# Five score blocks of an attention kernel exponentiated on GpSimd as powers of two

## The chip, the cores and the metric

The kernel runs on one core of a Trainium2 chip. The metric is device time in microseconds (us) from launch to end. The engines named here are TensorE (PE: matrix products; PEld is its weight load), ScalarE (ACT: exponentials), VectorE (DVE: elementwise work), GpSimd (POOL: its own small instructions and some DMA issues) and SyncE (SP: most DMA issues). Each engine runs its own list of instructions strictly in order; semaphores tie the lists together. SBUF is the on-chip working memory of 128 partitions, PSUM the memory that TensorE writes, with eight banks of 128x512 fp32.

## What is computed

Two independent blocks over a sequence of 2048 rows and 512 channels, joined along the last axis.

```python
# A: attention with 32 heads of 16 channels
qkv = x @ wqkv
scores = einsum("bhqd,bhkd->bhqk", q, k) * (Dh ** -0.5)
p = softmax(scores)
a = einsum("bhqk,bhkd->bhqd", p, v) ... @ wo
# B: a 4-tap shift, a gate, a causal convolution as long as the sequence, a gate
kv = (k shifted and weighted by shift_k) * v
y = causal_conv(kv, ssm_k) + kv * ssm_D      # the reference does it by FFT
b = q * y
return concatenate([a, b], axis=-1)
```

The softmax is computed without subtracting a maximum: a row of exponentials is multiplied with the values and with a column of ones, and the sum that the ones give divides the result.

## The kernel before, in words

**Score blocks.** The 2048 x 2048 scores of 32 heads are cut into 2048 blocks of 128 keys by 512 queries (`NBLK`). A block is one matmul of 32 rows (`emit_qk`, L730) into one PSUM bank. Four heads that lie in the four 32-row strips of TensorE, at one block of queries, form a *head group*: 64 blocks, numbered one after another; there are 32 groups (`blk_group`). Scores leave TensorE already multiplied by log2(e) and by 2^16 (`QSCALE`, `OCT`), so a block needs 2 to the power score/2^16.

**Chunks.** Blocks are taken in chunks of two or three. Chunk T uses three PSUM banks, 0 to 2 or 3 to 5 by turns, so chunk T+2 needs the banks of chunk T back. One activation on ScalarE (L737) turns a whole chunk into bf16 exponentials in SBUF (`PT`). The first 70 chunks have two blocks; later ones have three, except those that leave the third bank to a projection, an output product or a transpose of the convolution (`form`, `next_unit`).

**Blocks on VectorE.** Some chunks give their last block to VectorE (`exp_on_dve`): the activation is then two blocks wide, and VectorE computes the power of two in six instructions, L756 (out of PSUM, which frees the bank), L759, L761, L763, L765 and L767, by splitting the number into exponent and fraction. Such a block is taken out of a later place in the order (`pick`), and its product with the values (PV) waits in `dve_wait` until the group's turn. `form` starts such a chunk when at least `DVE_GAP` chunks have gone by and VectorE's planned load is under `DVE_OPEN`.

**PV.** The product of exponentials and values (`emit_pv`, L798) accumulates a group over its 64 blocks in one PSUM bank. `emit_pv_dyn` decides when: a block that is computed elsewhere joins when its group is the current one and, by the planned times, its exponential is ready; what is emitted stands in TensorE's list in order. When a group is full, `finish_group` transposes it on VectorE (L822), divides and lays it up for the output product (L870), whose result VectorE copies to one of three `OUTA` slots (L882). The store of the slot is issued from POOL's list; the fourth copy waits for the first slot's store to be done.

**Convolution.** It is 128 steps of four channels and 16 lags each (`conv_lags`, L922), on TensorE, between the attention's products. Its operand `WR` is a ring of 13 rows, each a load of 512 KB from a scratch tensor, issued from SP's list. `PACE` is the planned least time from one lag to the next, in ns. After a block of channels VectorE copies the result (L938), TensorE transposes it and VectorE multiplies it by q (L964).

**The order.** The kernel writes out each engine's list ahead of time, with a small planner: every instruction has a planned cost (`cost=692.0` for a 128x512 pass on VectorE), `advance` and `commit_one` pick VectorE's next job by its due time, and the run time order is the planned one. DMA issues on POOL have no planned duration.

**Memory that the change touches.** `WKV[:, 1]` holds the projection weights of the values (`WV`), which are last read by L465 in the first 70 chunks. `WKV[:, 0]` is used again for `wo`, loaded by POOL after the last projection of the keys.

Of the kernel before, what the change touches and what calls it, by code (L numbers as in the profile page):

```python
# [54 lines left out]
DVE_GAP = 2  # L55
DVE_OPEN = 2500.0
DVE_END = 48
PACE = 366.0
LAG_NS = 130.0
PE_SLACK = 850.0  # L60
PV_NS = 260.0
DMA_NS = 5600.0
N_TAIL = 9
# [90 lines left out]
def bass_concat_heads__mha_block__ssm_conv_h3__prompt_kernel(  # L154
# [24 lines left out]
    def sb(name, shape, dt=BF16):  # L179
        return enter(nc.sbuf_tensor(name, shape, dt))  # L180
# [22 lines left out]
    EI = sb("EI", [128, 4, QB], INT32)  # L203
    EM = sb("EM", [128, 2, QB], FP32)
    EH = sb("EH", [128, 2, QB], FP32)
    JNK = sb("JNK", [128, 2], FP32)
    WK = WKV[:, 0, :, :]
    WV = WKV[:, 1, :, :]
    WOP = WKV[:, 0, :, :]
    wr_flat = WR[:, :, :].rearrange("p r w -> p (r w)")  # L210
    KZS = wr_flat[:, 0:4 * LKZ].rearrange("p (c m) -> p c m", c=4)
# [193 lines left out]
    vones = VAF[:, :, 0:H * VW].rearrange("p k (h e) -> p k h e", e=VW)  # L405
    pool.op(lambda e: e.memset(vones[:, :, :, DH:VW], 1.0))
    h_vaf1 = pool.op(lambda e: e.memset(VAF[:, :, H * VW:VROW], 1.0))
    h_kz0 = pool.op(lambda e: e.memset(KZS[:, :, S:S + PAD], 0.0))
    pool.op(lambda e: e.wait_ge(*h_xn[3]), inc=False)
    load_kv(7, h_xn[3])  # L410
# [262 lines left out]
        return BGB if n == 1 else PVB  # L673

    chunks, on_dve, chunk_of, taken, last_at = [], {}, {}, set(), {}
    flow = {"nxt": 0, "left": NBLK, "tail": [], "half": 0, "gap": 0, "NT": None}

    def steps_to(n):
        return (4 * KT * n - flow["nxt"]) / 3.0
# [8 lines left out]
                            return b  # L688
        return None

    def new_chunk(T, n, dv=None):
        bl = []
        while len(bl) < n - (dv is not None):
            if flow["nxt"] not in taken:
                bl.append(flow["nxt"])
                last_at[blk_group(flow["nxt"])] = T
            flow["nxt"] += 1
        if dv is not None:
            b = pick(dv, [i % 4 for i in bl])
            if b is None:  # L700
                while flow["nxt"] in taken:
                    flow["nxt"] += 1
                b = flow["nxt"]
                last_at[blk_group(b)] = T
                flow["nxt"] += 1
            else:
                taken.add(b)
                on_dve[b] = len(on_dve)
                blk_on_dve[on_dve[b]] = b
            bl.append(b)  # L710
        for j, b in enumerate(bl):
            chunk_of[b] = (T, j)
        flow["left"] -= len(bl)
        chunks.append((bl, [3 * (T % 2) + i for i in range(len(bl))]))
# [4 lines left out]
    def emit_qk(T):  # L719
        bl, banks = chunks[T]  # L720
        deps = []
        for b, bank in zip(bl, banks):
            qb, g, kt, s = blk(b)
            deps += [h_q[(qb, g)], h_k[(g // 2, kt // 4)] if g > 1 or kt else h_k0, bank_free[bank]]

        def fn(e):
            ins = None
            for b, bank in zip(bl, banks):
                qb, g, kt, s = blk(b)
                ins = e.matmul(PS[:, bank, :],  # L730
                               lhsT=KTo[32 * s:32 * s + 32, g // 2, kt * 128:(kt + 1) * 128],
                               rhs=QT[32 * s:32 * s + 32, qb % 2, g, :],
                               start=True, stop=True, tile_position=(32 * s, 0))
            return ins
        h = pe_op(fn, deps, [("row", b % 4, 512) for b in bl])
        n = len(bl) - (bl[-1] in on_dve)
        h_exp[T] = act.op(lambda e: e.activation(PT[:, T % R_PT, 0:n * QB],  # L737
                                                 PS[:, banks[0]:banks[0] + n, :].rearrange("p b f -> p (b f)"),
                                                 ACT.Exp, scale=math.log(2.0) / OCT),
                          [h, h_ptfree.get(T - R_PT)], cost=n * QB / 1.2 + 87.0)  # L740
        for b, bank in zip(bl[:n], banks):
            bank_free[bank] = h_blk[b] = h_exp[T]
        if n < len(bl):
            bank_free[banks[n]] = exp_on_dve(bl[n], banks[n], h, T)

    h_fix = {}
    h_ptd = {}
    h_pair = {}

    def exp_on_dve(b, bank, h, T):  # L750
        i = on_dve[b]
        y, w = EM[:, i % 2, :], EH[:, i % 2, :]
        ei = EI[:, i % 4, :]
        f = ei.bitcast(UINT16).rearrange("p (n h) -> p n h", h=2)[:, :, 0]
        end = at_of(h_exp[T])
        h_fix[i] = job(lambda e: e.tensor_scalar(ei, PS[:, bank, :], FIX_LO, FIX_ADD, ALU.max, ALU.add),  # L756
                       [h, h_pair.get(i - 4)], 692.0, end)
        due = end + 7000.0
        js = [job(lambda e: e.scalar_tensor_tensor(y, f, 2.0 ** -32, f, ALU.mult, ALU.mult),  # L759
                  [h_fix[i], h_pair.get(i - 2)], 693.0, due - 3100.0)]  # L760
        js.append(job(lambda e: e.scalar_tensor_tensor(w, f, PC * 2.0 ** -16, y, ALU.mult, ALU.add),  # L761
                      [js[0]], 693.0, due - 2400.0))
        js.append(job(lambda e: e.tensor_scalar(ei, ei, 0x00ff0000, 7, ALU.bitwise_and, ALU.logical_shift_left),  # L763
                      [js[1]], 427.0, due - 1700.0))
        js.append(job(lambda e: e.scalar_tensor_tensor(w, w, PD, ei.bitcast(FP32), ALU.add, ALU.mult),  # L765
                      [js[2]], 693.0, due - 1300.0))
        js.append(job(lambda e: e.scalar_tensor_tensor(PTD[:, i % 4, :], y, PB, w, ALU.add, ALU.mult),  # L767
                      [js[3], (lambda: h_ptd.get(i - 4, WAIT)) if i >= 4 else None], 693.0, due))
        h_pair[i] = h_blk[b] = js[-1]
        passes.extend(js)  # L770
        dve_wait.append(b)
        return h_fix[i]
# [11 lines left out]
    def emit_pv(bl, T):  # L784
        deps = [h_blk[b] for b in bl] + [h_v[blk(b)[2]] for b in bl]
        for b in bl:
            qb, g, kt, s = blk(b)
            if kt == 0:
                deps.append(bank_free[pvb(qb * NG + g)])

        def fn(e):
            ins = None
            for b in bl:
                qb, g, kt, s = blk(b)
                h = 8 * (g // 2) + 2 * s + (g % 2)
                Tc, j = chunk_of[b]
                rhs = PTD[:, on_dve[b] % 4, :] if b in on_dve else PT[:, Tc % R_PT, j * QB:(j + 1) * QB]
                ins = e.matmul(PS[32 * s:32 * s + 32, pvb(qb * NG + g), :],  # L798
                               lhsT=VAF[:, kt, h * VW:h * VW + 32],
                               rhs=rhs,  # L800
                               start=(kt == 0), stop=(kt == KT - 1), tile_position=(0, 32 * s))
            return ins
        h = pe_op(fn, deps, [("col", b % 4, 512) for b in bl])
        for b in bl:
            if b in on_dve:
                h_ptd[on_dve[b]] = h
            else:
                h_ptfree[chunk_of[b][0]] = h
            n = blk_group(b)
            pv_left[n] -= 1  # L810
            if not pv_left[n]:
                finish_group(n, h, T)
# [327 lines left out]
    def form(T):  # L1140
        if flow["tail"]:
            new_chunk(T, flow["tail"].pop(0))
            return None
        if flow["left"] <= 27:
            plan_tail(T + 12)
            flow["tail"] = [3] * (flow["left"] - 24) + [2] * (36 - flow["left"])
            new_chunk(T, flow["tail"].pop(0))
            return None
        if T < T_DYN:
            new_chunk(T, 2)  # L1150
            return None
        flow["gap"] += 1
        u = next_unit(T)
        if u and (u[0] <= 4 or flow["gap"] >= 4):
            flow["gap"] = 0
            new_chunk(T, 2)
            return u[1:]
        while passes and passes[0].h is not None:
            passes.pop(0)
        load = sum(j.cost - 60.0 for j in passes if j.h is None)  # L1160
        if T >= flow["half"] and T >= T_DVE and load < DVE_OPEN and flow["left"] > DVE_END:
            v = (load + 4700.0) / 1270.0 * 1.1 + 3
            n = blk_group(min(flow["nxt"] + int(3 * v), NBLK - 1))
            if pick(n, [flow["nxt"] % 4, (flow["nxt"] + 1) % 4]) is not None:
                flow["half"] = T + DVE_GAP
                new_chunk(T, 3, n)
                return None
        new_chunk(T, 3)
        return None

    T = -1
    while flow["NT"] is None or T < flow["NT"] + 2:
# [7 lines left out]
            if u:  # L1180
                run_unit(T, *u)
        if T >= 2:
            pv_queue.extend(b for b in chunks[T - 2][0] if b not in on_dve) if T - 2 < len(chunks) else None
        emit_pv_dyn(T)
        if T < T_DYN:
            if early and early[0][0] <= T:
                t = max(max(Mm.tile), pe.t)
# [79 lines left out]
```

## Time and profile before

The median of three runs is 890.4 us (887.86 to 891.84). The profiled execution took 887.32 us.

| | before |
|---|---|
| profiled execution | 887.32 us |
| its span, first to last instruction | 885.6 us |
| ACT busy | 861.8 us, 97% |
| DVE busy | 823.7 us, 93% |
| PE busy | 714.2 us, 81% |
| POOL busy | 37.7 us, 4% |
| activations over a chunk (L737) | 727 |
| blocks on VectorE (L756) | 184 |
| mean granted TensorE clock | 0.972 |
| moved by DMA | 295.62 MB |

How to read it: a row of instructions gives the line of the kernel, the engine, the operation, output <- input by name, the shape (partitions x elements, type), the count, the busy time in us, the mean ns of one, and after the bar the idle time of its engine just ahead of it with what ended most of that. In a view of waits a row names who waited, for whom, the us in all, the times and the longest. In a timeline the first column is the start in us, the second the duration. In the view of one line the durations are min/median/max in ns, and then come the first and the last start.

### The profile page before, as it was taken

How to read it: one execution, taken by the hardware profiler on the slowest of the kernel's cores; microseconds unless marked ns; L12 is line 12 of the kernel's file. 1: busy time of each engine (PE TensorE's matmuls, PEld its weight loads, DVE VectorE, ACT ScalarE, POOL GpSimd, SP SyncE). 2: the span in 40 equal slices, each digit the busy share in tenths (PEclk: the TensorE clock that was granted, in tenths of full speed). 3: DMA queues.
4: the chain of work that ended last, by engine and by line, in shares of the span. 5: the costliest groups of instructions: out<-in, count | busy, mean ns of one | idle time of the engine just before them, and what ended most of it. 6: DMA issues, size and time to landing. Idle time of an engine off the chain costs nothing.

```text
span 885.6 us, 28864 instructions
## 1 busy us (share of the span) xinstructions
PE 714.2 (81%) x12754; PEld 321.8 (36%) x12798; DVE 823.7 (93%) x1422; ACT 861.8 (97%) x733; POOL 37.7 (4%) x60
## 2 busy tenths in 40 slices
PE   8988979778787878777788887778778877877787
PEld 3322334333333334333343333334333433333331
DVE  3888999999999999999999999999999999999971
ACT  6999999999999999999999999999999999999996
POOL 3132000000000000000001000000000000000000
PEclk9999999998999999999999999998999999999995
DMA  9876699999999999999999999999999999999920
GB/s 315 284 258 230 198 366 346 387 368 342 362 356 371 378 358 357 352 366 357 347 351 368 353 403 361 362 365 328 375 362 360 372 367 367 352 358 373 357 91 30
DMA packets 88430, 295.62 MB, mean 334 GB/s; under 512 B 11125, under 2 KB 19314, under 8 KB 87922
## 3 DMA queue, kind: packets, MB, share of 16 engines
q1 hardware_dynamic: 82386, 280.00, 86.8%
q0 software_dynamic: 3776, 12.58, 4.1%
q8 instruction: 102, 1.67, 0.7%
q10 hardware_dynamic: 2144, 1.18, 0.5%
q14 instruction: 22, 0.18, 0.1%
HBM read 287.31 MB, written 6.42 MB: 332 GB/s over the span
## 4 chain that ended last, share of the span: by engine, by line
ACT 68%; DVE 21%; PE 10%; issue 1%; ACTq 0%; DVEq 0%
ACT PT L737 67%; PE PS L730 4%; DVE EH L765 3%; DVE EI L756 3%; DVE EH L761 3%; DVE EM L759 3%; DVE PTD L767 3%; DVE EI L763 2%; PE PS L798 1%; PE PS L465 1%; PE PS L922 1%; PE PS L458 1%; DVE QT L486 1%; PE PS L870 1%; DVE YB L938 1%
## 5 line engine op out<-in xcount | busy, mean ns | idle before, releaser
L737 ACT ACTIVATE PT<-PS 128x1536 bf16<-128x1536 f32 (+1 forms) x727 | 858.2, 1382 | 11.4 <-PE PS L730 10.3
L730 PE MATMUL PS<-QT,KTo 32*128 32x512 bf16 x2048 | 292.3, 391 | 153.9 <-ACT PT L737 134.1
L922 PE MATMUL PS<-WR,KV 128*10 128x128 bf16 (+15 forms) x8192 | 270.8, 225 | 3.8 <-issue 2.4
L922 PEld LDWEIGHTS PS<-WR,KV 128*11 128x11 bf16 (+15 forms) x8192 | 192.0, 108 | 90.8 <-issue 50.1
L798 PE MATMUL PS<-PT,VAF 128*32 128x512 bf16 x1864 | 201.8, 398 | 0.6 <-ACT PT L737 0.3
L730 PEld LDWEIGHTS PS<-QT,KTo 32*128 32x128 bf16 x2048 | 72.4, 91 | 290.2 <-ACT PT L737 252.5
L765 DVE SCALAR_TENSOR_TENSOR EH<-EH,EI 128x512 f32<-128x512 f32 x184 | 131.2, 713 | 1.9
L759 DVE SCALAR_TENSOR_TENSOR EM<-EI 128x512 f32<-128x512 uint16 x184 | 131.5, 715 | 0.1
L761 DVE SCALAR_TENSOR_TENSOR EH<-EI,EM 128x512 f32<-128x512 uint16 x184 | 129.3, 703 | 1.1
L756 DVE TENSOR_SCALAR EI<-PS 128x512 int32<-128x512 f32 x184 | 127.5, 693 | 1.5 <-PE PS L730 1.2
L767 DVE SCALAR_TENSOR_TENSOR PTD<-EM,EH 128x512 bf16<-128x512 f32 x184 | 128.5, 699 | 0.4
L798 PEld LDWEIGHTS PS<-PT,VAF 128*32 128x32 bf16 x1864 | 49.9, 93 | 115.2 <-issue 106.2
L763 DVE TENSOR_SCALAR EI<-EI 128x512 int32<-128x512 int32 x184 | 81.0, 440 | 2.1
L798 PE MATMUL PS<-PTD,VAF 128*32 128x512 bf16 x184 | 63.2, 395 | 0.8 <-DVE PTD L767 0.3
L822 DVE STREAM_TRANSPOSE DT<-PS 128x512 f32<-128x512 f32 x31 | 22.9, 740 | 22.4 <-PE PS L798 21.6
L313 POOL DMA_DIRECT2D out_dram<-OUTA x12 | 7.0, 586 | 516.3 <-DVE OUTA L882 516.3
L938 DVE CAST YB<-PS 128x512 bf16<-128x512 f32 x32 | 21.9, 685 | 1.2 <-PE PS L922 0.4
L486 DVE TENSOR_TENSOR QT<-PS,MSK 128x1024 bf16<-128x1024 f32 x15 | 18.5, 1231 | 4.3 <-PE PS L451 4.3
L798 PEld LDWEIGHTS PS<-PTD,VAF 128*32 128x32 bf16 x184 | 15.4, 95 | 14.0 <-DVE PTD L767 7.1
L870 PE MATMUL PS<-WKV,OTN 128*128 128x512 bf16 x51 | 17.3, 436 | 2.4 <-issue 1.7
L502 DVE CAST VAF<-PS 128x512 bf16<-128x512 f32 x16 | 11.0, 690 | 7.8 <-PE PS L465 7.7
L465 PE MATMUL PS<-WKV,xT 128*128 128x512 bf16 x58 | 15.2, 381 | 1.0 <-issue 0.8
(71 smaller groups left out, 253.9 us busy)
## 6 DMA issues: line engine op xcount, KB each, us to landing
WR<-kz_scratch SPq DMA_DIRECT2D x512, 512.0 KB, 7.8
WR<-in_B_k_dram POOLq DMA_DIRECT2D x15, 256.0 KB, 7.5
kz_scratch<-WR SPq DMA_DIRECT2D x1, 2176.0 KB, 8.6
out_dram<-QN POOLq DMA_DIRECT2D x2, 1024.0 KB, 9.0
QT<-in_B_k_dram POOLq DMA_DIRECT2D x7, 256.0 KB, 8.8
KV<-in_A_x_dram SPq DMA_DIRECT2D x3, 512.0 KB, 8.5
out_dram<-OUTA POOLq DMA_DIRECT2D x12, 128.0 KB, 5.7
WR<-in_B_v_dram SPq DMA_DIRECT2D x5, 256.0 KB, 4.9
```

What stands on the lines that cost most here:

```text
L486: hh = dve_job(lambda e: e.tensor_tensor(QT[:, qb % 2, 2 * o:2 * o + 2, :], src, MSK[:, :, 0:1].broadcast_to([128, 2, QB]), ALU.mult), [h, ...
L730: ins = e.matmul(PS[:, bank, :], lhsT=KTo[32 * s:32 * s + 32, g // 2, kt * 128:(kt + 1) * 128], rhs=QT[32 * s:32 * s + 32, qb % 2, g, :], ...
L737: h_exp[T] = act.op(lambda e: e.activation(PT[:, T % R_PT, 0:n * QB], PS[:, banks[0]:banks[0] + n, :].rearrange("p b f -> p (b f)"), ACT.E ...
L756: h_fix[i] = job(lambda e: e.tensor_scalar(ei, PS[:, bank, :], FIX_LO, FIX_ADD, ALU.max, ALU.add), [h, h_pair.get(i - 4)], 692.0, end)
L759: js = [job(lambda e: e.scalar_tensor_tensor(y, f, 2.0 ** -32, f, ALU.mult, ALU.mult), [h_fix[i], h_pair.get(i - 2)], 693.0, due - 3100.0)]
L761: js.append(job(lambda e: e.scalar_tensor_tensor(w, f, PC * 2.0 ** -16, y, ALU.mult, ALU.add), [js[0]], 693.0, due - 2400.0))
L763: js.append(job(lambda e: e.tensor_scalar(ei, ei, 0x00ff0000, 7, ALU.bitwise_and, ALU.logical_shift_left), [js[1]], 427.0, due - 1700.0))
L765: js.append(job(lambda e: e.scalar_tensor_tensor(w, w, PD, ei.bitcast(FP32), ALU.add, ALU.mult), [js[2]], 693.0, due - 1300.0))
L767: js.append(job(lambda e: e.scalar_tensor_tensor(PTD[:, i % 4, :], y, PB, w, ALU.add, ALU.mult), [js[3], (lambda: h_ptd.get(i - 4, WAIT)) ...
L798: ins = e.matmul(PS[32 * s:32 * s + 32, pvb(qb * NG + g), :], lhsT=VAF[:, kt, h * VW:h * VW + 32], rhs=rhs, start=(kt == 0), stop=(kt == K ...
L922: ins = e.matmul(PS[32 * c:32 * c + NB - n, BGB, 128 * (kk % 4):128 * (kk % 4) + 128], lhsT=KV[:, n:NB, d], rhs=WR[:, d % R_W, 128 * (NB - ...
L938: bank_free[BGB] = dve_job(lambda e: e.tensor_copy(YB[:, half, :].rearrange("p (k i) -> p k i", k=4), src), [h, (lambda: h_yb.get(qd // 8 ...
```

## The change

In five chunks, the first at chunk 120 or soon after and the next ones at least 100 chunks apart, the third block is taken from two head groups ahead. VectorE copies its scores from PSUM to an fp32 tile in SBUF (`EG`), times 1/2^16; that copy frees the bank. GpSimd then computes 2 to the power of it, element by element, with a column of twos (`TWO`) as the base, into a bf16 tile (`PTG`, two slots). Both tiles lie in the memory of the value projection's weights. The planner counts 40 us for a power (`POW_NS`), and puts the block's PV into TensorE's list when the group's turn has come and that time has gone by. `feed_pool` puts a power into POOL's list once its copy stands in VectorE's. `PACE` goes from 366 to 363.

```diff
--- before.py
+++ after.py
@@ -55,9 +55,12 @@
 DVE_GAP = 2
 DVE_OPEN = 2500.0
 DVE_END = 48
-PACE = 366.0
+PACE = 363.0
 LAG_NS = 130.0
 PE_SLACK = 850.0
+POW_FIRST = 120
+POW_GAP = 100
+POW_NS = 40000.0
 PV_NS = 260.0
 DMA_NS = 5600.0
 N_TAIL = 9
@@ -203,9 +206,12 @@
     EI = sb("EI", [128, 4, QB], INT32)
     EM = sb("EM", [128, 2, QB], FP32)
     EH = sb("EH", [128, 2, QB], FP32)
+    TWO = sb("TWO", [128, 1], FP32)
     JNK = sb("JNK", [128, 2], FP32)
     WK = WKV[:, 0, :, :]
     WV = WKV[:, 1, :, :]
+    EG = WKV[:, 1, 0:2, :].rearrange("p a d -> p (a d)").bitcast(FP32).rearrange("p (a d) -> p a d", a=1)
+    PTG = WKV[:, 1, 2:4, :]
     WOP = WKV[:, 0, :, :]
     wr_flat = WR[:, :, :].rearrange("p r w -> p (r w)")
     KZS = wr_flat[:, 0:4 * LKZ].rearrange("p (c m) -> p c m", c=4)
@@ -405,6 +411,7 @@
     vones = VAF[:, :, 0:H * VW].rearrange("p k (h e) -> p k h e", e=VW)
     pool.op(lambda e: e.memset(vones[:, :, :, DH:VW], 1.0))
     h_vaf1 = pool.op(lambda e: e.memset(VAF[:, :, H * VW:VROW], 1.0))
+    h_two = pool.op(lambda e: e.memset(TWO[:, :], 2.0))
     h_kz0 = pool.op(lambda e: e.memset(KZS[:, :, S:S + PAD], 0.0))
     pool.op(lambda e: e.wait_ge(*h_xn[3]), inc=False)
     load_kv(7, h_xn[3])
@@ -673,7 +680,7 @@
         return BGB if n == 1 else PVB
 
     chunks, on_dve, chunk_of, taken, last_at = [], {}, {}, set(), {}
-    flow = {"nxt": 0, "left": NBLK, "tail": [], "half": 0, "gap": 0, "NT": None}
+    flow = {"nxt": 0, "left": NBLK, "tail": [], "half": 0, "gap": 0, "NT": None, "gnext": POW_FIRST}
 
     def steps_to(n):
         return (4 * KT * n - flow["nxt"]) / 3.0
@@ -688,7 +695,7 @@
                             return b
         return None
 
-    def new_chunk(T, n, dv=None):
+    def new_chunk(T, n, dv=None, gp=False):
         bl = []
         while len(bl) < n - (dv is not None):
             if flow["nxt"] not in taken:
@@ -705,8 +712,11 @@
                 flow["nxt"] += 1
             else:
                 taken.add(b)
-                on_dve[b] = len(on_dve)
-                blk_on_dve[on_dve[b]] = b
+                if gp:
+                    on_pool[b] = len(on_pool)
+                else:
+                    on_dve[b] = len(on_dve)
+                    blk_on_dve[on_dve[b]] = b
             bl.append(b)
         for j, b in enumerate(bl):
             chunk_of[b] = (T, j)
@@ -733,7 +743,7 @@
                                start=True, stop=True, tile_position=(32 * s, 0))
             return ins
         h = pe_op(fn, deps, [("row", b % 4, 512) for b in bl])
-        n = len(bl) - (bl[-1] in on_dve)
+        n = len(bl) - (bl[-1] in on_dve or bl[-1] in on_pool)
         h_exp[T] = act.op(lambda e: e.activation(PT[:, T % R_PT, 0:n * QB],
                                                  PS[:, banks[0]:banks[0] + n, :].rearrange("p b f -> p (b f)"),
                                                  ACT.Exp, scale=math.log(2.0) / OCT),
@@ -744,10 +754,31 @@
             bank_free[banks[n]] = exp_on_dve(bl[n], banks[n], h, T)
 
     h_fix = {}
+    on_pool, h_blk_g = {}, {}
     h_ptd = {}
     h_pair = {}
 
+    g_wait, g_free = [], {}
+
+    def exp_on_pool(b, bank, h, T):
+        i = on_pool[b]
+        eg = EG[:, 0, :]
+        j = job(lambda e: e.tensor_scalar(eg, PS[:, bank, :], 1.0 / OCT, None, ALU.mult), [h, h_blk_g.get(i - 1)], 692.0, at_of(h_exp[T]))
+        g_wait.append((i, b, eg, j))
+        h_blk[b] = Job(None, (), 0.0, 0.0)
+        dve_wait.append(b)
+        return j
+
+    def feed_pool():
+        while g_wait and g_wait[0][3].h is not None:
+            i, b, eg, j = g_wait.pop(0)
+            h = pool.op(lambda e: e.tensor_tensor(PTG[:, i % 2, :], TWO[:, 0:1].broadcast_to([128, QB]), eg, ALU.pow),
+                        [j.h, h_two, h_ptd.get(("g", i - 2))], cost=POW_NS)
+            h_blk[b].h = h_blk_g[i] = h
+
     def exp_on_dve(b, bank, h, T):
+        if b in on_pool:
+            return exp_on_pool(b, bank, h, T)
         i = on_dve[b]
         y, w = EM[:, i % 2, :], EH[:, i % 2, :]
         ei = EI[:, i % 4, :]
@@ -794,7 +825,7 @@
                 qb, g, kt, s = blk(b)
                 h = 8 * (g // 2) + 2 * s + (g % 2)
                 Tc, j = chunk_of[b]
-                rhs = PTD[:, on_dve[b] % 4, :] if b in on_dve else PT[:, Tc % R_PT, j * QB:(j + 1) * QB]
+                rhs = PTD[:, on_dve[b] % 4, :] if b in on_dve else PTG[:, on_pool[b] % 2, :] if b in on_pool else PT[:, Tc % R_PT, j * QB:(j + 1) * QB]
                 ins = e.matmul(PS[32 * s:32 * s + 32, pvb(qb * NG + g), :],
                                lhsT=VAF[:, kt, h * VW:h * VW + 32],
                                rhs=rhs,
@@ -804,6 +835,8 @@
         for b in bl:
             if b in on_dve:
                 h_ptd[on_dve[b]] = h
+            elif b in on_pool:
+                h_ptd[("g", on_pool[b])] = h
             else:
                 h_ptfree[chunk_of[b][0]] = h
             n = blk_group(b)
@@ -1158,6 +1191,12 @@
         while passes and passes[0].h is not None:
             passes.pop(0)
         load = sum(j.cost - 60.0 for j in passes if j.h is None)
+        if T >= flow["gnext"] and T >= flow["half"] and flow["left"] > 4 * DVE_END:
+            n = blk_group(flow["nxt"]) + 2
+            if n < NQB * NG and pick(n, [flow["nxt"] % 4, (flow["nxt"] + 1) % 4]) is not None:
+                flow["gnext"] = T + POW_GAP
+                new_chunk(T, 3, n, True)
+                return None
         if T >= flow["half"] and T >= T_DVE and load < DVE_OPEN and flow["left"] > DVE_END:
             v = (load + 4700.0) / 1270.0 * 1.1 + 3
             n = blk_group(min(flow["nxt"] + int(3 * v), NBLK - 1))
@@ -1180,8 +1219,10 @@
             if u:
                 run_unit(T, *u)
         if T >= 2:
-            pv_queue.extend(b for b in chunks[T - 2][0] if b not in on_dve) if T - 2 < len(chunks) else None
+            pv_queue.extend(b for b in chunks[T - 2][0] if b not in on_dve and b not in on_pool) if T - 2 < len(chunks) else None
+        feed_pool()
         emit_pv_dyn(T)
+        feed_pool()
         if T < T_DYN:
             if early and early[0][0] <= T:
                 t = max(max(Mm.tile), pe.t)
```

## The prediction

> **What bounds the kernel now.** I began with the page: the busy shares and the chain of waits.
>
> ```profile
> span 885.6 us, 28864 instructions
> ...
> PE 714.2 (81%) x12754; PEld 321.8 (36%) x12798; DVE 823.7 (93%) x1422; ACT 861.8 (97%) x733; POOL 37.7 (4%) x60
> ...
> ACT 68%; DVE 21%; PE 10%; issue 1%; ACTq 0%; DVEq 0%
> ```
>
> ScalarE (ACT) is busy for 97% of the span and holds 68% of the chain; VectorE (DVE) is close behind; GpSimd (POOL) is nearly empty. An average hides stages, so next come the windows of 100 us (busy time and instruction count of PE, PEld, DVE, ACT, POOL, then granted clock, DMA share, GB/s):
>
> ```profile
> 0.00:100.00 100.00, 89.01 (x610) 30.64 (x622) 77.50 (x134) 89.33 (x91) 26.07 (x44) 0.98 0.78 261
> 100.00:200.00 100.00, 81.21 (x1627) 38.28 (x1631) 97.52 (x167) 99.84 (x85) 0.76 (x1) 1.00 0.95 351
> 200.00:300.00 100.00, 81.90 (x1606) 38.37 (x1609) 98.35 (x170) 98.80 (x83) 2.23 (x4) 0.97 0.99 363
> 300.00:400.00 100.00, 77.46 (x1586) 37.12 (x1581) 98.25 (x172) 99.39 (x83) 0.00 (x0) 0.98 0.98 358
> 400.00:500.00 100.00, 80.77 (x1533) 37.81 (x1537) 97.01 (x167) 99.06 (x83) 4.80 (x6) 0.97 0.98 354
> 500.00:600.00 100.00, 78.21 (x1595) 37.91 (x1594) 98.16 (x171) 100.00 (x83) 0.00 (x0) 0.99 1.01 372
> 600.00:700.00 100.00, 80.91 (x1597) 38.20 (x1606) 97.62 (x169) 98.79 (x84) 2.23 (x4) 0.98 0.97 355
> ```
>
> From 100 us on ACT is 99 to 100% busy and DVE 97 to 98%: two full engines that share the exponentials. The ACT waits between 100 and 850 us confirm it: 3.9 us in all, from TensorE.
>
> ```profile
> ACT PT L737 <- PE PS L730: 3.9, 9, 0.6
> ```
>
> So the steady stage is worth what ACT and DVE are relieved of, and nothing else. The groups by shape give prices (columns: count, busy us, mean ns of one):
>
> ```profile
> L737 ACT ACTIVATE PT<-PS 128x1536 bf16<-128x1536 f32 x410 | 604.3, 1584 | 3.6 <-PE PS L730 3.1
> L737 ACT ACTIVATE PT<-PS 128x1024 bf16<-128x1024 f32 x317 | 343.9, 1121 | 7.9 <-PE PS L730 7.2
> ...
> L759 DVE SCALAR_TENSOR_TENSOR EM<-EI 128x512 f32<-128x512 uint16 x184 | 131.5, 715 | 0.1
> L765 DVE SCALAR_TENSOR_TENSOR EH<-EH,EI 128x512 f32<-128x512 f32 x184 | 131.2, 713 | 1.9
> L761 DVE SCALAR_TENSOR_TENSOR EH<-EI,EM 128x512 f32<-128x512 uint16 x184 | 129.3, 703 | 1.1
> L767 DVE SCALAR_TENSOR_TENSOR PTD<-EM,EH 128x512 bf16<-128x512 f32 x184 | 128.5, 699 | 0.4
> L756 DVE TENSOR_SCALAR EI<-PS 128x512 int32<-128x512 f32 x184 | 127.5, 693 | 1.5 <-PE PS L730 1.2
> L763 DVE TENSOR_SCALAR EI<-EI 128x512 int32<-128x512 int32 x184 | 81.0, 440 | 2.1
> ```
>
> One block less in an activation saves 1584 - 1121 = 463 ns by the means, or 604.3/410 - 343.9/317 = 389 ns by busy time, where overlapping activations count once. I take 0.43 us. A block on DVE costs (131.5 + 131.2 + 129.3 + 128.5 + 127.5 + 81.0)/184 = 3.96 us.
>
> **The change part by part.** *Five activations of three blocks become two blocks wide.* Chunks stay three blocks long, so their number hardly moves; ACT loses 5 x 0.43 = 2.1 us, all on the path. The rule of the code (chunk 120, then every 100, while over 192 blocks are left) might admit a sixth block, worth 0.3 us net; I keep five.
>
> *Five copies on DVE.* PSUM to SBUF, 128x512, one input: the nearest row is L756, 693 ns, so 5 x 0.69 = 3.5 us. DVE is full, so this displaces 3.5/3.96 = 0.87 of a block, which returns to ACT: +0.4 us. The copy also frees the PSUM bank, as L756 does for a DVE block, at the same place in the order; no new wait there.
>
> *Five powers on GpSimd.* The trace shows no power. Its only elementwise rows are
>
> ```profile
> L397 POOL TENSOR_SCALAR_AFFINE_SELECT MSK<-MSK 128x8 f32<-128x8 f32 x2 | 0.4, 189 | 0.1
> ...
> L403 POOL TENSOR_SCALAR_AFFINE_SELECT IDN<-IDN 128x128 bf16<-128x128 bf16 x1 | 0.3, 294 | 0.0
> ```
>
> (294 - 189)/120 = 0.88 ns per element, or 0.19 + 504 x 0.00088 = 0.63 us for 512: the low bound. No row bounds it from above. The written order allows 40 us: no PV (the product of the exponentials with the values) of such a block is put into TensorE's queue sooner. Anywhere between 0.63 and 40 us the path pays nothing, so the sum needs no value. The cover is the wait for the block's group: a group lasts about 27 us by the transposes below, and the block lies two groups ahead. If that cover is gone, TensorE stands in order before this PV, with the next scores behind it, and ACT starves about a chunk later.
>
> ```profile
> L822 DVE STREAM_TRANSPOSE DT<-PS x31: 697/718/911, 71.5 to 878.8; 128x512 f32<-128x512 f32 x31
> ```
>
> *What queues behind a power on POOL.* The windows' ACT counts, less four instructions at the start that are no chunks, give 87 chunks by 100 us, then 172, 255, 338, 421, 504, 588. With a few chunks lost to conditions that are not yet met, powers are due near chunks 122, 223, 324, 425 and 527: about 141, 261, 383, 505 and 627 us. Beside them stand POOL's own DMA issues (start, duration):
>
> ```profile
> 158.44 0.76 POOL L313 DMA_DIRECT2D WKV<-in_A_wo_dram  x1 [59.67 <-PE PS L458]
> 255.74 0.56 POOL L313 DMA_DIRECT2D out_dram<-OUTA  x1 [96.54 <-DVE OUTA L882]
> 260.33 0.56 POOL L313 DMA_DIRECT2D out_dram<-OUTA  x1 [4.04 <-DVE OUTA L882]
> 264.88 0.57 POOL L313 DMA_DIRECT2D out_dram<-OUTA  x1 [3.99 <-DVE OUTA L882]
> 269.58 0.54 POOL L313 DMA_DIRECT2D out_dram<-OUTA  x1 [4.12 <-DVE OUTA L882]
> 462.19 0.54 POOL L313 DMA_DIRECT2D out_dram<-OUTA  x1 [192.07 <-DVE OUTA L882]
> ...
> 492.69 1.45 POOL L313 DMA_DIRECT2D QN<-in_B_q_dram  x1 [11.04 <-DMA out_dram<-QN]
> 685.60 0.76 POOL L313 DMA_DIRECT2D out_dram<-OUTA  x1 [191.46 <-DVE OUTA L882]
> ```
>
> With 40 us each, the first power holds the load of wo from 158 to about 182; its first reader ends in the store at 255.7. The second holds two or three stores until about 302; their OUTA slots are wanted again near 461. The fourth follows the load at 492.7, and the fifth ends at 667, ahead of 685.6. Cost: nothing, up to about 55 us per power.
>
> *PACE 366 to 363.* The convolution's 2048 lags (8192 matmuls, four per lag) may end 2048 x 3 ns = 6.1 us sooner.
>
> ```profile
> L922 PE MATMUL PS<-WR,KV x8192: 216/219/327, 98.3 to 854.7; 128*3 128x128 bf16 x16, 128*6 128x128 bf16 x15, 128*15 128x128 bf16 x14, 128*16 128x128 bf16 x13
> ...
> L737 ACT ACTIVATE PT<-PS x727: 997/1462/1915, 9.1 to 877.0; 128x1536 bf16<-128x1536 f32 x109, 128x1024 bf16<-128x1024 f32 x73
> ```
>
> It ends at 854.7, the exponentials' last start is at 877.0: it is covered and gains nothing. Its loads must come 0.8% faster: the mean of the six windows from 100 to 700 us, 359 GB/s, becomes 362, and the window at 500 us already carried 372.
>
> *The sum.* -2.1 + 0.4 = -1.7 us (bounds -1.5 and -2.0 by the two prices of a block). The profiled execution took 887.32 us, the span and 1.7 us around it: 885.6. It stands 3.1 us under the median of 890.4, so on the median's scale the forecast is 888.7, 0.2% less.
>
> **A rule against this change.** The powers read SBUF for as long as they last, beside a DVE that is 98% busy, mostly with operations of two SBUF inputs. The nearest thing in the trace is POOL issuing the store at 255.74, beside these rows (start, duration):
>
> ```profile
> 255.36 0.68 DVE L767 SCALAR_TENSOR_TENSOR PTD<-EM,EH 128x512 bf16<-128x512 f32 x1
> 255.96 0.71 DVE L761 SCALAR_TENSOR_TENSOR EH<-EI,EM 128x512 f32<-128x512 uint16 x1
> ```
>
> 0.68 and 0.71 us against means of 699 and 703 ns: no stretch. But an issue reads no tile, so this row excludes little. The Trainium skill (SBUF — State Buffer, "Who interferes with whom") says that a DVE instruction with two SBUF inputs and a GpSimd instruction that reads SBUF contend for one read interface, and that whichever starts first keeps it for its whole length while the other stands still. No run here shows it; by that rule the sum would be that of the first rival.
>
> **The rivals.** *VectorE is shut out while a power runs (slower).* Place: the four two-input lines L759, L761, L765, L767, and everything behind them in DVE's order. With 184 DVE chunks among some 640, a bank that only DVE frees is needed every three or four chunks, and its next use is two chunks on, so ACT lasts four chunks of about 1.2 us (100/83), say 5 us. Price: 5 x (D - 5) for a power of D us. At 0.63 us it costs nothing; it decides from about D = 6; at 40 it is 175 us, 1064 in all. For it: DVE's share of two-input work. Against: the rows above, which are weak. Only D near the allowance makes this large. Chance 0.09.
>
> *The power outlasts its allowance (slower).* By the chunk numbers above the blocks lie in groups 6, 10, 15, 20 and 24, and all but one (group 20) have begun when 40 us are over, so the PV comes at once, with about 3 us to spare. Price 4 x (D - 43): D = 45 gives 897, D = 50 gives 917; beyond 55 the fifth power also delays the store at 685.6. For: nothing in the trace bounds D. Against: the nearest row is sixty times shorter. Chance 0.08.
>
> *The block only takes the place of a DVE block.* DVE chunks come when its load is small enough; if each power pushes one out for good, ACT gets those five blocks back and nothing is gained: 890.4. For: the new test stands ahead of DVE's. Against: the load that it goes by stays small, and DVE's chunk is formed right after. That the change does less than it says belongs here. Chance 0.09.
>
> *The new order closes ACT's remaining gaps (faster).* All later chunks are laid out anew. ACT idles 11.5 us before L737 (3.6 + 7.9). Half of it closed gives 890.4 - 1.7 - 5.7 = 883. For: changed order changes small waits. Against: only 3.9 us of it lie in the steady stage, the rest at start and tail, which hardly change. Chance 0.09.
>
> *The loads fall behind the quicker pace.* All 6.1 us return as TensorE waits: about 895 at the worst. Against: no wait on these loads is listed. Chance 0.04.
>
> **How the numbers follow.** The forecast, 888.7, has 0.61. About 0.5% (4.5 us) is what a measurement of this kernel tells from no change: its three runs lie 4 us apart. The forecast's own range is therefore 884 to 893; of its 0.61 I give 0.48 to within 0.5%, 0.11 to faster (a new order helping a little), 0.02 to slower. Faster: 0.11 + 0.09 = 0.20. Same: 0.48 + 0.09 and 0.01 of slow loads = 0.58. Slower: 0.02 + 0.09 + 0.08 + 0.03 = 0.22. Since cases of both signs hold weight, the range reaches from the filled gaps, 882, to a power just over its allowance, 899 (D about 45.5), and leaves out most of the first rival, the longer powers and a little below.
>
> **What would show it.** In the changed profile: five POOL groups of 128x512 with a PV from their tile; 1024-wide activations up by about five; ACT still 99% in the windows. Five or more gaps in ACT of the length of a power, beside a stretched L759 or L765, mean the first rival; TensorE waiting on POOL, the second; fewer than 183 DVE blocks, the third; L922 waiting on DMA, the last. I am wrong if the steady windows show a full ACT and a time outside 884 to 893.

## The result, and the profile after

The changed kernel takes 1123.55 us (median of four runs, 1120.36 to 1128.45) where the kernel before takes 890.03: a ratio of 1.264, 95% interval 1.261 to 1.267. The forecast was 888.7. The profiled execution has a span of 1122.8 us, 237.2 more than before.

The page of the changed kernel, its busy shares and its chain of waits:

```profile
span 1122.8 us, 28907 instructions
...
PE 724.2 (64%) x12763; PEld 324.8 (29%) x12806; DVE 826.0 (74%) x1428; ACT 861.6 (77%) x733; POOL 531.4 (47%) x67
...
POOL 44%; DVE 26%; ACT 17%; PE 10%; issue 3%; ACTq 0%; POOLq 0%; DVEq 0%
```

ACT is busy for as long as before (861.6 us against 861.8) and DVE too (826.0 against 823.7). Next to no work was added to them (six copies of 0.68 us on DVE); they stand still for longer. GpSimd, which was not on the chain at all, holds 44% of it. The groups of instructions (in the changed file L775 is the power, L766 the copy ahead of it, L740 the scores, L747 the activation, L829 the PV):

```profile
L747 ACT ACTIVATE PT<-PS 128x1536 bf16<-128x1536 f32 (+1 forms) x727 | 858.1, 1388 | 249.4 <-PE PS L740 248.6
L775 POOL TENSOR_TENSOR WKV<-TWO,WKV 128x512 bf16<-128x512 f32 x6 | 494.2, 82370 | 281.1 <-DVE WKV L766 281.1
...
L829 PE MATMUL PS<-WKV,VAF 128*32 128x512 bf16 x6 | 3.6, 608 | 231.5 <-POOL WKV L775 231.5
```

There are six powers, not five, and each takes 82.4 us where the written order allows 40. ACT's idle time ahead of its activations grew from 11.5 to 249.4 us. The waits say for whom (waiter, released by, us in all, times, longest):

```profile
ACT PT L747 <- PE PS L740: 248.6, 36, 42.4
...
PE PS L829 <- POOL WKV L775: 231.5, 6, 42.0
DVE EI L787 <- PE PS L740: 193.9, 11, 42.4
```

Six times TensorE stands before the one PV whose exponentials GpSimd still computes, 231.5 us in all. The next scores are behind it in TensorE's order, so ACT and DVE run dry. One of the six in windows, the second power (which ran from 303.4 to 385.5 us), with the columns of the windows before:

```profile
303.00:344.00 41.00, 32.45 (x677) 15.39 (x670) 40.05 (x70) 40.78 (x35) 40.58 (x1) 1.00 1.01 367
344.00:385.00 41.00, 0.00 (x0) 0.00 (x0) 1.06 (x3) 1.50 (x2) 41.00 (x1) 0.53 0.12 48
385.00:391.00 6.00, 5.45 (x62) 1.89 (x66) 3.66 (x6) 3.66 (x3) 1.07 (x2) 0.50 0.19 62
```

The first half of the power is free: ACT is busy for 40.8 of 41 us, DVE for 40.1 of 41. The second half is a standstill of everything, the loads included (a DMA share of 0.12), since the convolution on TensorE stands too and frees no row of the ring `WR`. In the 6 us after it TensorE's granted clock is 0.50, and the six PV that ended the waits took 608 ns against 400 for the others. So 231.5 us of the 237.2 between the two profiles (233.5 between the medians) are the wait. The rest fits slow restarts of about 1 us each; no run tests that.

### The profile page after: what moved, and what is told of

Its sections match the earlier page's. It is cut to its first block, busy times and chain, and to the rows that moved or that the text cites. A ratio compares the mean times of both kernels' runs of the same rounds, so it can differ in the third digit from the quotient of the medians.

```text
span 1122.8 us, 28907 instructions
## 1 busy us (share of the span) xinstructions
PE 724.2 (64%) x12763; PEld 324.8 (29%) x12806; DVE 826.0 (74%) x1428; ACT 861.6 (77%) x733; POOL 531.4 (47%) x67
## 3 DMA queue, kind: packets, MB, share of 16 engines
q10 hardware_dynamic: 2144, 1.18, 0.4%
## 4 chain that ended last, share of the span: by engine, by line
POOL 44%; DVE 26%; ACT 17%; PE 10%; issue 3%; ACTq 0%; POOLq 0%; DVEq 0%
POOL WKV L775 44%; ACT PT L747 17%; DVE EH L792 4%; DVE EH L796 4%; DVE EI L787 4%; DVE EM L790 4%; DVE PTD L798 4%; PE PS L740 3%; DVE EI L794 2%; PE PS L829 2%; PE PS L955 2%; PE PS L472 1%; PE PS L465 1%; DVE QT L493 1%; DVE DT L855 1%
## 5 line engine op out<-in xcount | busy, mean ns | idle before, releaser
L747 ACT ACTIVATE PT<-PS 128x1536 bf16<-128x1536 f32 (+1 forms) x727 | 858.1, 1388 | 249.4 <-PE PS L740 248.6
L775 POOL TENSOR_TENSOR WKV<-TWO,WKV 128x512 bf16<-128x512 f32 x6 | 494.2, 82370 | 281.1 <-DVE WKV L766 281.1
L740 PE MATMUL PS<-QT,KTo 32*128 32x512 bf16 x2048 | 294.5, 393 | 148.5 <-ACT PT L747 129.2
L955 PE MATMUL PS<-WR,KV 128*14 128x128 bf16 (+15 forms) x8192 | 271.6, 227 | 1.5 <-DVE YB L971 0.7
L787 DVE TENSOR_SCALAR EI<-PS 128x512 int32<-128x512 f32 x184 | 127.6, 693 | 194.2 <-PE PS L740 193.9
L955 PEld LDWEIGHTS PS<-WR,KV 128*10 128x10 bf16 (+15 forms) x8192 | 193.0, 108 | 84.0 <-issue 46.1
L829 PE MATMUL PS<-PT,VAF 128*32 128x512 bf16 x1858 | 201.7, 400 | 2.1 <-DVE DT L855 1.3
L740 PEld LDWEIGHTS PS<-QT,KTo 32*128 32x128 bf16 x2048 | 72.4, 91 | 289.1 <-ACT PT L747 244.6
L829 PE MATMUL PS<-WKV,VAF 128*32 128x512 bf16 x6 | 3.6, 608 | 231.5 <-POOL WKV L775 231.5
L829 PEld LDWEIGHTS PS<-PT,VAF 128*32 128x32 bf16 x1858 | 49.7, 93 | 119.1 <-issue 107.8
L829 PE MATMUL PS<-PTD,VAF 128*32 128x512 bf16 x184 | 66.6, 398 | 2.8 <-DVE PTD L798 1.6
L829 PEld LDWEIGHTS PS<-WKV,VAF 128*32 128x32 bf16 x6 | 0.6, 101 | 233.4 <-POOL WKV L775 233.4
L915 DVE CAST OUTA<-PS 128x512 bf16<-128x512 f32 x12 | 8.4, 696 | 45.5 <-PE PS L903 45.4
L319 POOL DMA_DIRECT2D out_dram<-QN x2 | 2.4, 1200 | 59.2 <-DVE EI L794 55.3
L319 POOL DMA_DIRECT2D WR<-in_B_k_dram x15 | 11.0, 735 | 29.9 <-DVE KV L566 21.0
```

The lines of the kernel that those rows point to most:

```text
L740: ins = e.matmul(PS[:, bank, :], lhsT=KTo[32 * s:32 * s + 32, g // 2, kt * 128:(kt + 1) * 128], rhs=QT[32 * s:32 * s + 32, qb % 2, g, :], ...
L775: h = pool.op(lambda e: e.tensor_tensor(PTG[:, i % 2, :], TWO[:, 0:1].broadcast_to([128, QB]), eg, ALU.pow), [j.h, h_two, h_ptd.get(("g", ...
L955: ins = e.matmul(PS[32 * c:32 * c + NB - n, BGB, 128 * (kk % 4):128 * (kk % 4) + 128], lhsT=KV[:, n:NB, d], rhs=WR[:, d % R_W, 128 * (NB - ...
```

## The experiments

Theory 1: the whole loss is TensorE waiting, because a power takes twice its allowance. Theory 2, the first rival of the prediction in any strength: a power burdens VectorE or the memory while it runs.

### The length of a power, in the same order

Two runs keep the written order to the instruction and raise fewer columns to the power, so that the rest of the block is left out; one replaces the power by a multiplication. The three + lines below are these three runs, one line each.

```diff
-  e.tensor_tensor(PTG[:, i % 2, :], TWO[:, 0:1].broadcast_to([128, QB]), eg, ALU.pow)
+  e.tensor_tensor(PTG[:, i % 2, 0:384], TWO[:, 0:1].broadcast_to([128, 384]), eg[:, 0:384], ALU.pow)
+  e.tensor_tensor(PTG[:, i % 2, 0:256], TWO[:, 0:1].broadcast_to([128, 256]), eg[:, 0:256], ALU.pow)
+  e.tensor_tensor(PTG[:, i % 2, :], TWO[:, 0:1].broadcast_to([128, QB]), eg, ALU.mult)
```

384 columns:

> The changed kernel in the very same order, with 384 of the 512 columns raised to a power and the rest left as the tile held it. Theory 1: by the element a power takes 61.7 us; in the written order the six PV stand 46, 40.5, 41, 52, 41 and 44 us behind the copies, so TensorE waits 6 x 61.7 - 265 = 106 us in all, and the time is about 996. If the loss were a burden in proportion to the powers' length: three quarters of 235 us, 1064.

256 columns:

> The changed kernel in the very same order, but GpSimd raises only 256 of the 512 columns of each block to a power; the other half keeps what the tile held before. Theory 1: if a power costs by the element, it takes 41 us; the PV stand 40 to 52 us behind the copy in the written order, so TensorE waits 0 to 2 us per power, 3 us in all, and the time is 889 to 893. Theory 2: half of the 235 us lost, about 1007.

The multiplication:

> The changed kernel in the very same order, with a multiplication in place of the power (the result is then not an exponential). Theories 1 and 2 alike: a GpSimd operation of about 1 us, far inside the allowance; what is left is the gain that the prediction summed, for six blocks 6 x 0.34 = 2.0 us: about 888, ratio 0.998 (0.996 to 1.000). If it stays slower than before by several us, the copies or the new order cost something by themselves.

Measured, the 384 columns took 997.6 us (one run). Its group of powers, and TensorE's wait for them:

```profile
L775 POOL TENSOR_TENSOR WKV<-TWO,WKV 128x384 bf16<-128x384 f32 x6 | 371.8, 61973 | 278.3 <-DVE WKV L766 278.3
```

```profile
PE PS L829 <- POOL WKV L775: 107.9, 6, 21.8
```

The 256 columns took 890.98 us, ratio 1.004 (1.001 to 1.007), with the same two rows:

```profile
L775 POOL TENSOR_TENSOR WKV<-TWO,WKV 128x256 bf16<-128x256 f32 x6 | 249.3, 41558 | 291.3 <-DVE WKV L766 291.3
```

```profile
PE PS L829 <- POOL WKV L775: 2.5, 2, 1.3
```

The multiplication took 887.46 us, ratio 0.9998 (0.9972 to 1.0023):

```profile
L775 POOL TENSOR_TENSOR WKV<-TWO,WKV 128x512 bf16<-128x512 f32 x6 | 8.8, 1469 | 367.3 <-DVE WKV L766 367.3
```

A power costs by the element: 41.56, 61.97 and 82.37 us for 256, 384 and 512 columns, 161 to 162 ns a column, while a multiplication of the same shape takes 1.47 us in all. TensorE's wait is not in proportion to that: 2.5, 107.9 and 231.5 us. It is what sticks out beyond the 40 to 52 us that stand between copy and PV in this order (in the run with the multiplication, where nothing waits, the six distances are 45.6, 40.1, 41.2, 52.0, 41.4 and 43.7 us), as theory 1 has it to within 2 us (expected 106 for 384 columns); a burden in proportion would have given 1064 us there. Halving the power took the loss away almost whole.

### An order that allows 84 us

Two ways to mend it. The first changes the allowance alone and leaves the blocks two head groups ahead. For both, the product that closes a strip's sum is found by counting, since a late block can now be the last of its strip.

```diff
-POW_NS = 40000.0
+POW_NS = 84000.0
...
-                               start=(kt == 0), stop=(kt == KT - 1), tile_position=(0, 32 * s))
+                               start=(kt == 0), stop=ends[b], tile_position=(0, 32 * s))
```

> The changed kernel with the allowance put right, 84 us, and the blocks still two head groups ahead (with the small change to the last product of a strip). Theory 1: no wait of TensorE for GpSimd's powers; but a group that is 55 to 73 us away at its end is complete but for this one block before the power is done, and the next group has no bank to begin in. The wait moves into the written order: 10 to 25 us a power, 80 us in all, about 970. If two groups were far enough: 890.

It took 968.6 us, as expected in size, but not in form. The waits of that run, where L835 is the PV:

```profile
ACT PT L747 <- PE PS L740: 93.4, 40, 27.5
...
PE PS L835 <- POOL WKV L775: 63.1, 5, 21.2
```

TensorE still stands before five of the six PV. When the whole group is done but for that block, the planner puts the block into TensorE's list early rather than run out of exponential slots, and the wait takes place there. Three stores also stood behind the fifth power, and VectorE waited 23.1 us for one of them, most of it while TensorE stood as well. Two head groups are too near for 82 us, whatever the allowance says.

The second keeps the allowance of 84 us, takes the block three groups ahead, early in a group, and starts powers at least 80 chunks apart and only in stretches of chunks (`POW_AT`) behind which no store or load stands on GpSimd's queue. That leaves four of them.

```diff
-            n = blk_group(flow["nxt"]) + 2
-            if n < NQB * NG and pick(...) is not None:
+            n = blk_group(flow["nxt"]) + 3
+            if n < NQB * NG and flow["nxt"] % 64 < 30 and any(p <= T < q for p, q in POW_AT) and pick(...) is not None:
```

> The changed kernel with four powers instead of six, each allowed 84 us in the written order, its block taken three head groups ahead, and begun where no store or load of GpSimd's queue stands behind it (a small change lets the last product of a strip close its sum, whichever block that is). Theory 1 (the whole loss is TensorE standing before the PV, because a power takes 82.3 us where 40 were allowed): no wait of TensorE for GpSimd over 2 us, and 4 x (0.43 - 0.07) = 1.4 us less than before, so about 888.5, ratio 0.998. Theory 2 (the power also burdens VectorE or the memory while it runs): the 4 x 82 = 329 us in which a power runs show longer two-input operations on VectorE, and the time stays above before by as much; a tenth of slowing would be 30 us, 920.

It took 892.27 us, ratio 1.0046 (1.0017 to 1.0074). No wait of TensorE for a power is listed. Windows of that run, with a power (the first and the third row) and without:

```profile
301.00:383.00 82.00, 62.31 (x1319) 30.38 (x1320) 80.46 (x140) 81.69 (x68) 81.85 (x1) 1.00 0.99 360
385.00:512.00 127.00, 105.22 (x1970) 48.01 (x1967) 124.16 (x213) 125.86 (x105) 4.56 (x6) 0.95 0.99 366
513.00:595.00 82.00, 65.13 (x1342) 31.34 (x1339) 80.93 (x140) 81.71 (x69) 82.00 (x1) 0.98 1.00 367
```

ACT finishes 68 and 69 activations in 82 us beside a power, 105 in 127 us without one: 0.83 to 0.84 per us everywhere. VectorE's four two-input lines, first within the power from 301 to 383 us, then between 385 and 512 us:

```profile
L799 DVE SCALAR_TENSOR_TENSOR PTD<-EM,EH 128x512 bf16<-128x512 f32 x21 | 15.2, 724 | 0.1
L793 DVE SCALAR_TENSOR_TENSOR EH<-EI,EM 128x512 f32<-128x512 uint16 x20 | 14.2, 711 | 0.1
L797 DVE SCALAR_TENSOR_TENSOR EH<-EH,EI 128x512 f32<-128x512 f32 x20 | 14.1, 704 | 0.2
L791 DVE SCALAR_TENSOR_TENSOR EM<-EI 128x512 f32<-128x512 uint16 x20 | 14.1, 703 | 0.0
```

```profile
L797 DVE SCALAR_TENSOR_TENSOR EH<-EH,EI 128x512 f32<-128x512 f32 x31 | 22.1, 713 | 0.3
L791 DVE SCALAR_TENSOR_TENSOR EM<-EI 128x512 f32<-128x512 uint16 x31 | 21.9, 706 | 0.0
L793 DVE SCALAR_TENSOR_TENSOR EH<-EI,EM 128x512 f32<-128x512 uint16 x31 | 21.3, 689 | 0.2
L799 DVE SCALAR_TENSOR_TENSOR PTD<-EM,EH 128x512 bf16<-128x512 f32 x30 | 21.1, 705 | 0.0
```

In the mean of the four lines that is 711 ns beside the power and 703 without. Over all four powers of the run it is 706 ns, between them 699, and in the same stretches of the kernel before 707 and 706. VectorE is not shut out for a power's length; if it is slowed at all, it is by about 1%. The 230 us are gone; but the run is 0.5% above before where 0.2% below was expected. That rest is taken up below.

### Powers in the way of GpSimd's stores

The same with powers wherever a spacing of 80 chunks puts them, without the stretches.

> The same with powers wherever the spacing puts them: seven, of which the second, the fourth and the sixth start shortly before a cluster of four stores that GpSimd issues. Theory 1 with GpSimd's queue: the stores stand behind a power, the fourth copy to OUTA waits for the first store, and VectorE stands for about 60 us in each of three clusters: 888 + 180 = about 1070, with no wait of TensorE for GpSimd's powers. If the queue did not matter: 888. Theory 2: as in the run with four powers, more by the ratio 7 to 4.

It took 1062.5 us (one run). GpSimd's list around the second power (start, duration), and what VectorE waited for (L922 is the copy to OUTA):

```profile
246.53 82.32 POOL L775 TENSOR_TENSOR WKV<-TWO,WKV 128x512 bf16<-128x512 f32 x1 [21.45 <-DVE WKV L766]
328.82 1.68 POOL L319 DMA_DIRECT2D out_dram<-OUTA  x3
331.97 0.54 POOL L319 DMA_DIRECT2D out_dram<-OUTA  x1 [1.47 <-DVE OUTA L922]
```

```profile
DVE OUTA L922 <- DMA out_dram<-OUTA: 173.4, 3, 61.0
```

Three stores leave together when the power ends, and the fourth copy has waited for the first. Three clusters, 173.4 us: with no late PV left, a second mechanism costs nearly as much as the first. An engine that only issues stores now and then is not free for 82 us at a time.

### The last half per cent

Three runs ask what the rest is: the powers beside the others, the quicker pace, or the new order by itself.

The order of the run with four powers, with a multiplication in place of each power:

> The run with four powers that fit, in the very same order, with a multiplication in place of each power. If the new order makes its 0.4 to 0.5%: the same ratio, 1.004 to 1.006. If the powers do, by running beside: 1.000 or less, down to the 0.998 that the sum of the prediction would give.

893.18 us, ratio 1.006 (1.003 to 1.009). The powers are not what holds that order above before.

The same order with four powers and the old pace (`PACE` 363 to 366):

> The run with four powers that fit, with PACE put back to 366. In that run ScalarE's waits for scores had already grown, from 1.9 to 4.4 us between 70 and 145 us, before the first power began, and half as many columns or a mere multiplication showed the same. If the quicker pace of the convolution makes those waits: about 4 us less than with 363, ratio to before about 0.999. If the powers themselves cost the 4 us: unchanged, ratio 1.004 to 1.005.

893.93 us, ratio 1.0064 (1.0033 to 1.0095). The pace is not what holds that order above before either.

The old kernel with the new pace, and with the closing product found by counting:

> The kernel before with PACE 363 and nothing else of the change (with the same small change to the last product of a strip as in the run with four powers). If the quicker pace costs: 3 to 5 us more than before, ratio 1.003 to 1.006. If it is covered, as the prediction had it: no difference, ratio 0.998 to 1.002.

892.96 us, ratio 1.0037 (1.0010 to 1.0064): slightly above before. But the run with the multiplication in the order of the changed kernel has the same pace and a ratio of 0.9998, so the pace by itself is not shown to cost anything.

The old order, with six powers that nobody waits for in GpSimd's list:

```diff
+    def idle_powers(n):
+        for i in range(n):
+            h_one[0] = pool.op(lambda e, i=i: e.tensor_tensor(PTG[:, i, :], TWO[:, 0:1].broadcast_to([128, QB]), EG, ALU.pow), [h_two, h_one[0]])
...
+            if i in (3, 11):
+                idle_powers({3: 2, 11: 1}[i])
```

(one more behind the load of wo, two behind the load of q.)

> The kernel before, its order on every other engine untouched, with six powers of 128x512 put into GpSimd's list between its DMA issues, on a tile of its own; nobody waits for them and nothing stands behind them in time. They run for 6 x 82 = 494 us. If a power burdens VectorE by shutting out its two-input operations for its length: hundreds of us. If it burdens the other engines a little (the 0.4% that the hidden powers seemed to cost): 4 to 6 us more than before, ratio 1.004 to 1.007. If the 0.4% is the new order: ratio 1.000 within 0.003.

892.65 us, ratio 1.0049 (1.0018 to 1.0080). The timeline of GpSimd at its last power, that of VectorE around the same moment, and the same VectorE line in the kernel before at about that time (start, duration):

```profile
703.17 81.96 POOL L866 TENSOR_TENSOR WKV<-TWO,WKV 128x512 bf16<-128x512 f32 x1
```

```profile
702.81 1.72 DVE L767 TENSOR_SCALAR EI<-EI 128x512 int32<-128x512 int32 x1
704.56 0.69 DVE L769 SCALAR_TENSOR_TENSOR EH<-EH,EI 128x512 f32<-128x512 f32 x1
```

```profile
703.11 0.52 DVE L763 TENSOR_SCALAR EI<-EI 128x512 int32<-128x512 int32 x1
```

The operation on VectorE at the power's start took 1.72 us instead of about 0.44; it ends 1.4 us after that start, and the next one, with two inputs, is back at 0.69 while the power goes on for 82 us. At each of the six powers one or two operations that read SBUF twice or from SBUF to SBUF are stretched so, by 0.3 to 1.5 us together, and end 1.3 to 1.9 us after the start. That makes some 5 us, as much as the run lies above before, so it may be a cause; the starts were not moved to test it. In the profiled execution it is hardly the whole: ScalarE waits 16.4 us for scores against 10.3 before, and 2.5 us of the growth (4.4 against 1.9) lie between 70 and 145 us, ahead of the first power at 161.75. In the run with four powers only one start shows a clear stretch:

```profile
300.74 0.69 DVE L788 TENSOR_SCALAR EI<-PS 128x512 int32<-128x512 f32 x1
301.34 1.17 DVE L799 SCALAR_TENSOR_TENSOR PTD<-EM,EH 128x512 bf16<-128x512 f32 x1
```

The power began at 300.91. The operation out of PSUM beside its start took its usual 0.69 us, the one with two inputs after it 1.17. The run with a multiplication in place of that power shows the same:

```profile
298.01 1.05 POOL L776 TENSOR_TENSOR WKV<-TWO,WKV 128x512 bf16<-128x512 f32 x1 [27.46 <-DVE WKV L767]
298.43 1.18 DVE L799 SCALAR_TENSOR_TENSOR PTD<-EM,EH 128x512 bf16<-128x512 f32 x1
```

A multiplication of 1.05 us stretches the operation as much as a power of 82 us, so the stretch does not grow with the length of the power. Why there is one the runs do not show.

What stays open: why every newly laid order of this kernel came out 0 to 0.6% slower and none faster. Neither the pace nor the powers explain it for the order with four powers, and for the six idle powers the stretches are not shown to explain it all; the runs do not tell more.

## Why the prediction was wrong

*What bounds the kernel*: right. ACT and DVE are full, and nothing but their standing still made the difference.

*Activations and copies*: about right, and irrelevant. Six blocks moved (404 activations of 1536 against 410; I kept five although the rule of the code allowed a sixth), the copy took 0.68 us. The gain of 1.7 us never showed: with a power that costs nothing (the multiplication) the ratio is 0.9998, and its interval holds both 0.998 and no change.

*The power on GpSimd* is the step that failed: "Anywhere between 0.63 and 40 us the path pays nothing, so the sum needs no value." The low bound came from a row, the high one from none. The 40 us are the planner's allowance; I let a constant of the written order stand as the end of the range. The power takes 82.4 us, 131 times the low bound. The nearest rows were a select, and neither they nor the three small additions on GpSimd (0.2 us each) bounded another operation.

*The second rival* was what happened, at 0.08. Its formula holds: 4 x (82.4 - 43) is 158 us; the block in group 20, with the 52 us measured between its copy and its PV, adds 30, and the sixth power a wait of 38.9, together 227; the trace has 231.5. The sign named for it, TensorE waiting on POOL, is the one that the trace shows. Mechanism, place and price were in the prediction; what was mis-sized is D, and with it the chance. "The nearest row is sixty times shorter" was no argument against it, since that row is no power. The range ended at D = 45.5 for the same reason.

*The first rival*, VectorE shut out: refuted by the run with four powers (706 ns beside them, 699 between) and by the changed kernel itself, whose DVE was busy 40.1 of 41 us in the first half of the second power. That the powers read SBUF for as long as they last was assumed there; no run shows it. With D = 82 the rival's price, 5 x (D - 5), would have been 385 us. The rule of the Trainium skill (SBUF — State Buffer, "Who interferes with whom"), by which the prediction set this rival, would have had two-input operations stand for each whole power; the runs show them held until 1.3 to 1.9 us after its start at most, so the measurement decides against it here.

*GpSimd's queue*: "nothing, up to about 55 us per power". With 41.6 us a power (the run with 256 columns) no wait for a store is listed, as forecast. In the changed kernel there is none either, but there the standstills had moved the stores against the powers. With the PV in time and 82 us a power the queue cost 173.4 us in three places, 58 us each. The mechanism was right.

*PACE covered*: not decided. In the order of the kernel before it came out 0.4% slower (0.1 to 0.6), where the prediction had nothing, and in the changed order with a multiplication 0.0%; since a new pace also lays the order anew, the runs do not say which of the two it was.

*The other rivals* did not come. 184 blocks still go to VectorE (L787). In the run with the multiplication ScalarE's waits for scores are 15.0 us against 10.3 before, so no gap was closed, and no wait of the convolution for a load is listed.

## What to carry to other kernels

When work is moved to an engine whose cost for that very operation has no row, the forecast is a price as a function of the unknown duration, and the chance of the far side cannot be argued down by a row of another operation. In a list that is run in order, an allowance that is too short by 40 us costs 40 us each time, and all engines pay it; look up at once how late the consumer may come and compare it with the longest duration that nothing excludes. A helper engine that also issues stores can delay them by as much as its longest instruction.

## What the runs showed of the hardware that was not expected

- GpSimd's power of two fp32 inputs costs 161 to 162 ns a column of 128 partitions (41.56 us for 256, 82.37 us for 512), 56 times a multiplication of the same shape (1.47 us).
- Beside such powers VectorE's two-input operations took 706 ns in the mean, between them 699. Only one or two operations at a power's start are stretched, in the worst case from 0.44 to 1.72 us, and a multiplication of 1.05 us does the same (1.18 us for an operation of about 0.70, against 1.17 at the start of a power).
- After 42 us of standing still TensorE's granted clock was 0.50 in the next 6 us, and the PV that ended the six waits took 608 ns instead of 400. In the run with 384 columns the PV behind waits of 10 to 22 us took the same 0.61 us.
